# Rows of x and W1 ordered by head: y turned by matmuls of 96 and 32 columns, and sent SBUF to SBUF into x from the fourth group on

## The chip, the cores and the metric

The kernel runs on one core of one Trainium2 chip. The metric is the device time of one execution in microseconds; the time before is 962.65 us, the median of three runs (960.43 to 962.67).

## What is computed

A recurrence with complex decay, for 4 batches, 8 heads, 768 steps and a head width of 48, feeds a mixture of four dense experts whose outputs are all summed with normalised weights:

```python
S_re, S_im = (new_re + kv, new_im)                 # per step t: state times a[t], plus k[t] v[t]^T
y[:, :, t] = np.einsum('bhd,bhde->bhe', q[:, :, t], S_re)
...
x = np.ascontiguousarray(attn_out.transpose(0, 2, 1, 3)).reshape(B * S, H * D)      # 3072 x 384
...
for e in range(E):                                 # E = 4, w1[e] is 384 x 1024, w2[e] 1024 x 384
    h = np.maximum(x @ w1[e], 0.0)
    out += p[:, e:e + 1] * (h @ w2[e])
```

A feature of x is (head, place in the head): 8 x 48 = 384, which fill NJ = 3 blocks of 128 partitions on the chip. The order of the features within x is free as long as the rows of W1 follow it.

## The kernel before

Everything is split by time into NG = 12 groups of G = 256 steps, each of CG = 2 chunks of C = 128. The kernel has two stages.

**First stage.** For each group, `front` prepares queries and keys on the vector engine (DVE) and the scalar engine (ACT), and `send` moves them between partitions by DMA, the pieces of 16 partitions on POOL's queue and the others on SP's. The attention of a group (`near_attention` for groups 0 and 1, `attention` after that) is matmuls in chunked form; its result y has 112 partitions, in which a pair of heads lies at partitions 0 to 47 and 64 to 111, four pairs (HP) beside each other. While that goes on, `moe1` runs the first two experts for the group before, in eight steps of `w1_step` and `w2_step`. The pieces are woven together by hand in `between` and `advance`: a group's attention is taken up at steps `FIRST` to `end`, and `hold` keeps the sends of the next group's queries back until then. What is not pinned by `behind` and `keep_in_program_order` a planner orders, over the whole kernel, by simulated times.

y has to become x: 128 features on the partitions in three blocks, split into a high and a low part (`split_x`, L229: xh on ACT, xl on DVE), which `w1_step` (L246) multiplies with W1. There are two ways:

- For groups 0 to 2 (g < XSEL = 3), `turn_x` (L700 to L710) does it by matmul: for each chunk and each block j the two pairs of heads that lie in the block are multiplied with a slice of `band`, a shifted identity, 128 columns wide, and added up in PSUM. `split_x` reads PSUM. y is stored to DRAM as well, by `store_y` (L749 to L752), in two DMAs, one for each half of the pairs.
- For groups 3 to 11, `store_y` writes y to `y_d[g]` in DRAM, and `load_x` (L224 to L226) reads it back into the tile x with 128 features on the partitions, which waits on SP until both stores have landed.

`band` is made at the start on POOL (L343 to L347: a memset and two affine selects). The tile x and `band` share one buffer.

**Second stage.** The other two experts read `y_d` (`load_x2`, L1126) in blocks of 768 steps and work on sums of blocks of x and W1 (a scheme with fewer products). Weights that it needs are partly prepared in the first stage and written to `late_d` (L824, L825). A slow general path for unusual inputs stands behind a flag and does not run here.

SP's queue and POOL's queue are worked off in order: a DMA whose input is not ready holds up those behind it. PE, ACT and DVE are each in order as well.

Of the kernel before, what the change touches and what calls it, by code (L numbers as in the profile page):

```python
# [8 lines left out]
F32 = mybir.dt.float32  # L9
F32R = mybir.dt.float32r  # L10
AF = mybir.ActivationFunctionType
ALU = mybir.AluOpType
# [3 lines left out]
B, H, S, D = 4, 8, 768, 48  # L16
HD = H * D
NT = B * S
E, F = 4, 1024
P = 128  # L20
NJ = HD // P
C = 128
G = 256
CG = G // C
NG = NT // G
GB = S // G
NF = E * F // P
FE = F // P
# [5 lines left out]
M = 112  # L34
IM = 64
# [14 lines left out]
HP = H // 2  # L50
# [8 lines left out]
XSEL = 3  # L59
# [2 lines left out]
STEP = {1: 4.2, 2: 4.2, 3: 4.2, 4: 4.2, 5: 4.2}  # L62
MORE = (1.5, 2.3, 0.5)
LATE = {NG - 1: (1, 2, 3, 4, 5, 6, 7), NG: (0,)}
HOFF = 96
ROWS = ((0, 48, (0, 1, 2), 0, 0), (48, 48, (0, 1, 2), 0, 3), (96, 32, (0, 1), 0, 6), (96, 16, (2,), 32, 6),
        (112, 16, (2,), 32, 7))
WIDE = 32 + P + 48
DMA_SCRATCH = 4096
XOF = (0, 1, 2, 3, 4, 5, 6, 7, 0, 8, 9, 6, 10, 11, 12, 13, 14, 15, 5, 9)  # L70
UNIT = (
# [54 lines left out]
def fast_path(ctx, tc, qkP, aP, vP, probsP, w, out, flag):  # L126
    nc = tc.nc
    const = ctx.enter_context(tc.tile_pool(name="const", bufs=1))
    wpool = ctx.enter_context(tc.tile_pool(name="wpool", bufs=NF1))
    moe = ctx.enter_context(tc.tile_pool(name="moe", bufs=2))  # L130
# [4 lines left out]
    wide = const.tile([P, WIDE], F32, name="wide")  # L135
    nc.gpsimd.memset(wide, 0.0)
    nc.gpsimd.affine_select(out=wide, in_=wide, pattern=[[-1, WIDE]], compare_op=ALU.not_equal, fill=1.0,
                            base=32, channel_multiplier=1)
# [82 lines left out]
            behind(ins, prev)  # L221
            prev = ins

    def load_x(g):  # L224
        x = moe.tile([P, NJ, G], F32, tag="x", name=f"xa{g}", bufs=1)
        nc.sync.dma_start(x, y_d[g].rearrange("(j p) t -> p j t", p=P))  # L226
        return [(slice(0, G), x)]

    def split_x(g, parts):  # L229
# [68 lines left out]
    with ExitStack() as c1:  # L298
# [38 lines left out]
        for t in Gs:  # L337
            nc.gpsimd.memset(t, 0.0)
        nc.gpsimd.memset(TA, 0.0)
        band = moe.tile([P, HOFF + P + IM + C], F32, tag="x", name="band", bufs=1)  # L340
        near_mask = band[:, HOFF + P + IM:]
        band = band[:M, :HOFF + P + IM]
        nc.gpsimd.memset(band, 0.0)  # L343
        nc.scalar.activation(near_mask, m_ps[:, 2], AF.Copy)
        for r0, base in ((0, HOFF), (IM, HOFF + D)):
            nc.gpsimd.affine_select(out=band[r0:r0 + D], in_=band[r0:r0 + D], pattern=[[-1, HOFF + P + IM]],
                                    compare_op=ALU.not_equal, fill=1.0, base=base, channel_multiplier=1)  # L347

        def landed_first(ins, prev):
            if prev is not None:  # L350
# [349 lines left out]
        def turn_x(g, c, y):  # L700
            xp = ps_a.tile([P, NJ, C], F32, tag="pa", name=f"xp{g}_{c}")
            for j in range(NJ):
                ps = [p for p in range(HP) if -HOFF < 2 * D * p - P * j < P]
                for p in ps:
                    o = HOFF - (2 * D * p - P * j)
                    ins = nc.tensor.matmul(xp[:, j, :], band[:, o:o + P], y[:, p, c * C:(c + 1) * C],  # L706
                                           start=(p == ps[0]), stop=(p == ps[-1]))
                    if g == 0 and c == 0 and p == ps[0]:
                        behind(ins, state["yl", g, 1])
            return slice(c * C, (c + 1) * C), xp  # L710

# [35 lines left out]
            rotate(g)  # L747

        def store_y(g, y):  # L749
            yv = y_d[g].rearrange("(p u d) t -> u d p t", u=2, d=D)  # L750
            for u in range(2):
                nc.sync.dma_start(yv[u], y[u * IM:u * IM + D])  # L752

        def attention(g, QK):
            y = small.tile([M, HP, G], F32, tag="y", name=f"y{g}", bufs=1)
            (turn0, _, inc0, sc0, val0), (turn1, _, inc1, sc1, val1) = (chunk(g, c, QK[1], y) for c in range(CG))
            turn0()
            sc1()
            sc0(joined=True)
            inc0(True)  # L760
            yield turn1()
            val0(True, begin=True)
            inc1(True)
            val1(True)
            t_factors(g)
            store_y(g, y)
            x = [turn_x(g, c, y) for c in range(CG)] if g < XSEL else load_x(g)
            rotate(g)
            yield x

# [113 lines left out]
        x = {}  # L884
# [456 lines left out]
def general_path(ctx, tc, qkT, aT, vt, probs, w, out):  # L1341
# [97 lines left out]
    with ExitStack() as c2:  # L1439
        sb = c2.enter_context(tc.tile_pool(name="g_sb2", bufs=1))  # L1440
        ps = c2.enter_context(tc.tile_pool(name="g_ps2", bufs=2, space=PSUM))
        wt = sb.tile([P, NF, 2 * HD], F32, name="g_w")
        for i in range(NF):
            nc.sync.dma_start(wt[:, i, :], w[i])
        NB = S // P
        for b in range(B):
            with tc.For_i(0, S, P) as t0:
                x = sb.tile([P, H, D], F32, name="g_x")
                nc.sync.dma_start(x, y_d[:, b, bass.ds(t0, P), :].rearrange("h t e -> t h e"))
                pr = sb.tile([P, E], F32, name="g_pr")  # L1450
                nc.sync.dma_start(pr, probs[b * S:(b + 1) * S, :][bass.ds(t0, P), :])
                prs = sb.tile([P, 1], F32, name="g_prs")
                nc.vector.reduce_sum(prs, pr, axis=mybir.AxisListType.X)
                nc.vector.tensor_scalar(prs, prs, 1e-9, None, op0=ALU.add)
                nc.vector.reciprocal(prs, prs)
                nc.vector.tensor_tensor(pr, pr, prs.broadcast_to([P, E]), op=ALU.mult)
                xf = x.rearrange("p h d -> p (h d)")
                xp = ps.tile([P, NJ, P], F32, name="g_xp")
                for j in range(NJ):
                    nc.tensor.transpose(xp[:, j, :], xf[:, j * P:(j + 1) * P], ident)  # L1460
                xs = sb.tile([P, NJ, P], F32, name="g_xs")
                nc.scalar.activation(xs, xp, AF.Copy)
                acc = sb.tile([P, HD], F32, name="g_acc")
                for e in range(E):
                    po = ps.tile([P, HD], F32, name="g_po")
                    for f in range(FE):
                        wi = wt[:, e * FE + f, :]
                        hp = ps.tile([P, P], F32, name="g_hp")
                        for j in range(NJ):
                            nc.tensor.matmul(hp, wi[:, j * P:(j + 1) * P], xs[:, j, :],  # L1470
                                             start=(j == 0), stop=(j == NJ - 1))
                        hs = sb.tile([P, P], F32, name="g_hs", bufs=2)
                        nc.scalar.activation(hs, hp, AF.Relu)
                        nc.tensor.matmul(po, hs, wi[:, HD:], start=(f == 0), stop=(f == FE - 1))
                    if e == 0:
                        nc.vector.tensor_scalar(acc, po, pr[:, e:e + 1], None, op0=ALU.mult)
                    else:
                        nc.vector.scalar_tensor_tensor(acc, po, pr[:, e:e + 1], acc, op0=ALU.mult, op1=ALU.add)
                ot = out[b * S:(b + 1) * S, :][bass.ds(t0, P), :].rearrange("(i s) d -> s i d", i=SEG)
                for s in range(CS):  # L1480
                    nc.sync.dma_start(ot[s], acc[s * SEG:(s + 1) * SEG, :])
# [62 lines left out]
```

## Time and profile before

| | before |
|---|---|
| median of three runs | 962.65 us (960.43 to 962.67) |
| profiled execution | 960.0 us, span 958.2 us |
| PE busy | 933.9 us, 97% of the span |
| PE weight loads busy (beside PE) | 908.3 us, 95% |
| DVE busy | 745.2 us, 78% |
| ACT busy | 483.0 us, 50% |
| POOL busy | 210.7 us, 22% |
| granted TensorE clock over the span | 0.999 of full speed |

Engine times overlap, so they do not add up to the span. PE's matmuls are pipelined: the time of one record includes its way through the engine, and records overlap, so the distance from start to start is the better measure of what one costs. Where rows are merged, the duration runs from the first start to the last end.

### The profile page before, as it was taken

The numbers are of one execution on the slowest core, as the hardware profiler recorded it, in microseconds if no ns is written. First come the engines' busy times: TensorE is split into PE (matmuls) and PEld (weight loads), VectorE is DVE, ScalarE is ACT, GpSimd is POOL, SyncE is SP. The second block draws the span as 40 slices with busy tenths as digits, with TensorE's granted clock in tenths as the row PEclk, the third lists the DMA queues.
The fourth block names the chain that finished last, engine by engine and source line by source line (L and its number), as shares of the span: only waits on it lengthen the run. The fifth ranks groups of instructions, "written<-read, shape, count | busy, mean of one in ns | idle before, by whom it ended". The sixth has DMA issues, their size and how long they took to land.

```text
span 958.2 us, 19409 instructions
## 1 busy us (share of the span) xinstructions
PE 933.9 (97%) x7388; PEld 908.3 (95%) x7388; DVE 745.2 (78%) x1630; ACT 483.0 (50%) x1030; POOL 210.7 (22%) x294
## 2 busy tenths in 40 slices
PE   5999999999999999999999999999999999999997
PEld 3899999999999999999999999999999999999997
DVE  7898989989989999888996577748485757666642
ACT  7766446363564736547343555635454554444430
POOL 6030111020211202111111036333424352322000
PEclk9999999999999999999999999999999999999999
DMA  9585264544535546353437799131514433131112
GB/s 314 171 172 139 60 159 89 150 99 142 149 96 129 129 138 156 117 135 109 117 109 226 269 316 275 50 121 38 148 57 144 162 85 102 50 99 51 50 50 78
DMA packets 75029, 125.73 MB, mean 131 GB/s; under 512 B 9600, under 2 KB 50224, under 8 KB 74928
## 3 DMA queue, kind: packets, MB, share of 16 engines
q1 hardware_dynamic: 60464, 94.69, 32.7%
q0 software_dynamic: 14464, 29.72, 13.3%
q8 instruction: 60, 0.98, 0.5%
q14 instruction: 41, 0.34, 0.1%
HBM read 75.94 MB, written 31.46 MB: 112 GB/s over the span
## 4 chain that ended last, share of the span: by engine, by line
PE 89%; DVE 6%; DMA 3%; ACT 2%; issue 1%; SPq 0%; ACTq 0%; DVEq 0%
PE ph L246 21%; PE pob L995 20%; PE po L267 19%; PE pb L995 17%; PE sc L635 3%; PE yp L667 2%; PE dp L611 2%; PE yp L677 2%; PE ktp L584 1%; DMA RX<-w 1%; PE sc L652 1%; DMA shi<-late_d 1%; DVE pf L446 1%; PE xp L706 1%; DVE xl L1001 0%
## 5 line engine op out<-in xcount | busy, mean ns | idle before, releaser
L995 PE MATMUL pob<-shi,hid 128*128 128x384 f32 x528 | 148.5, 335 | 0.5 <-DVE hid L1004 0.5
L267 PE MATMUL po<-whi,hh 128*128 128x384 f32 x384 | 129.7, 338 | 0.0
L267 PE MATMUL po<-wlo,hh 128*128 128x384 f32 x384 | 128.9, 336 | 0.0
L257 ACT ACTIVATE hh<-ph 128x512 fp32r<-128x512 f32 x96 | 57.2, 596 | 121.8 <-PE ph L246 117.5
L1007 POOL TENSOR_TENSOR Z<-Z 128x384 f32<-128x384 f32 x84 | 89.9, 1104 | 114.6 <-DMA Z<-y_d 57.0
L246 PE MATMUL ph<-xha,whi 128*128 128x256 f32 x576 | 103.8, 287 | 1.3 <-ACT xha L233 1.3
L246 PE MATMUL ph<-xla,whi 128*128 128x256 f32 x576 | 101.0, 283 | 2.0 <-DVE xla L235 2.0
L246 PE MATMUL ph<-xha,wlo 128*128 128x256 f32 x576 | 102.0, 284 | 0.0
L995 PE MATMUL pb<-xh,shi 128*128 128x384 f32 x291 | 97.1, 335 | 1.0 <-DVE pb L1001 1.0
L995 PEld LDWEIGHTS pob<-shi,hid 128*128 128x128 f32 x528 | 96.4, 188 | 1.2 <-DVE hid L1004 1.1
L995 PE MATMUL pb<-xl,shi 128*128 128x384 f32 x288 | 96.2, 334 | 0.0
L995 PE MATMUL pb<-xh,slo 128*128 128x384 f32 x288 | 96.2, 334 | 0.0
L246 PEld LDWEIGHTS ph<-xha,whi 128*128 128x128 f32 x576 | 85.9, 190 | 5.3 <-issue 2.4
L258 DVE SCALAR_TENSOR_TENSOR hl<-ph,hh 128x512 fp32r<-128x512 f32 x96 | 65.9, 687 | 31.0 <-ACT hh L257 30.3
L995 PE MATMUL pob<-slo,hid 128*128 128x384 f32 x264 | 88.2, 334 | 0.0
L267 PE MATMUL po<-whi,hl 128*128 128x384 f32 x384 | 85.2, 338 | 0.5 <-DVE hl L258 0.5
L246 PEld LDWEIGHTS ph<-xla,whi 128*128 128x128 f32 x576 | 82.8, 191 | 2.7 <-DVE xla L235 2.4
L246 PEld LDWEIGHTS ph<-xha,wlo 128*128 128x128 f32 x576 | 82.8, 190 | 0.4
L998 ACT ACTIVATE SN<-pb 128x384 f32<-128x384 f32 x96 | 47.4, 494 | 66.7 <-PE pb L995 59.4
L1001 DVE TENSOR_TENSOR xl<-Z,xh 128x384 fp32r<-128x384 f32 x104 | 59.2, 598 | 21.7 <-ACT xh L998 16.3
L998 ACT ACTIVATE hid<-pb 128x384 fp32r<-128x384 f32 x76 | 37.3, 491 | 71.9 <-PE pb L995 71.5
L267 PEld LDWEIGHTS po<-whi,hh 128*128 128x128 f32 x384 | 72.4, 189 | 0.3 <-ACT acc L775 0.2
(238 smaller groups left out, 2119.4 us busy)
## 6 DMA issues: line engine op xcount, KB each, us to landing
qk<-qkP SPq DMA_DIRECT2D x24, 384.0 KB, 4.0
acc_d<-acc POOLq DMA_DIRECT2D x24, 384.0 KB, 5.3
ACC<-acc_d SPq DMA_DIRECT2D x48, 192.0 KB, 3.2
A<-aP SPq DMA_DIRECT2D x22, 384.0 KB, 6.1
v<-vP SPq DMA_DIRECT2D x24, 288.0 KB, 3.0
Z<-y_d SPq DMA_DIRECT2D x16, 384.0 KB, 4.8
Qst<-Q SPq DMA_DIRECT2D x40, 145.1 KB, 3.9
Kst<-K SPq DMA_DIRECT2D x40, 144.0 KB, 3.8
```

What stands on the lines that cost most here:

```text
L246: ins = nc.tensor.matmul(ph[:, u, :], wt[:, j * P:(j + 1) * P], xt[:, j, :], start=(n == 0), stop=(n == 3 * NJ - 1))
L257: wts["hh"] = nc.scalar.activation(hh, ph, AF.Relu)
L258: nc.vector.scalar_tensor_tensor(hl, ph, 0.0, hh, op0=ALU.max, op1=ALU.subtract)
L267: nc.tensor.matmul(po[t], part[0][:, u, t * P:(t + 1) * P], wts[i][n][:, HD:], start=(i % FE == 0 and part[0] is hh and n == 0), stop=(i % ...
L611: ins = nc.tensor.matmul(d_ps[o:o + n, h, :], KT[:, c, h, o:o + n], vc[:, h * D:(h + 1) * D], start=True, stop=True)
L635: ins = nc.tensor.matmul(to, k, q, start=True, stop=True)
L667: ins = nc.tensor.matmul(yo, vc[:, vo:vo + n], scs[2 * c + h // 4][:, h % 4, :], start=True, stop=first)
L677: ins = nc.tensor.matmul(yo, st[:, o:o + n], Qc[:, o // D, :], start=False, stop=True)
L995: return tc.keep_in_program_order(nc.tensor.matmul(*args, **kw))
L998: return pin(nc.scalar.activation(dst, src, fn, scale=scale))
L1001: pin(nc.vector.tensor_tensor(dst, x, y, op=op))
L1007: nc.gpsimd.tensor_tensor(dst, x, y, op=op)
```

## The change

The features of x are put into a new order, and the rows of W1 into the same order on the host: block j begins with the 96 features of the j-th pair of heads, and its last 32 rows hold a part of the fourth pair. XROWS lists the pieces as (first row in y, rows, first and last pair, first row in x, block).

- `turn_x` now takes two matmuls for each block, one with 96 columns of `band` for the block's own pair, and one with 32 columns for the part of the fourth pair, each into its own partitions of PSUM and with nothing to add up. As before that is six for a chunk.
- For groups 3 to 11 y no longer goes through DRAM: `send_x` copies it by six DMAs from SBUF into the tile x, the two pieces of 16 rows on POOL's queue, the other four on SP's; x is then written to `y_d[g]` by one DMA from there, for the second stage. `load_x` is gone. `t_factors` stands behind the sends in the text.
- For groups 0 to 2 `store_y` needs six DMAs in place of two.
- `band` has another layout and is filled by six small copies on POOL out of an identity, in place of two affine selects; it is narrower.

```diff
+XROWS = ((0, 48, 0, 3, 0, 0), (64, 48, 0, 3, 48, 0), (0, 32, 3, 4, 96, 0), (64, 32, 3, 4, 96, 1), (32, 16, 3, 4, 96, 2),
+         (96, 16, 3, 4, 112, 2))
+XMAIN = 2 * D
...
-    def load_x(g):
+    def send_x(g, y):
         x = moe.tile([P, NJ, G], F32, tag="x", name=f"xa{g}", bufs=1)
-        nc.sync.dma_start(x, y_d[g].rearrange("(j p) t -> p j t", p=P))
+        for r, n, p0, p1, q, j in XROWS:
+            (nc.gpsimd if n == 16 else nc.sync).dma_start(x[q:q + n, j:j + p1 - p0, :], y[r:r + n, p0:p1, :])
+        nc.sync.dma_start(y_d[g].rearrange("(j p) t -> p j t", p=P), x)
         return [(slice(0, G), x)]
...
         nc.gpsimd.memset(band, 0.0)
         nc.scalar.activation(near_mask, m_ps[:, 2], AF.Copy)
-        for r0, base in ((0, HOFF), (IM, HOFF + D)):
-            nc.gpsimd.affine_select(out=band[r0:r0 + D], in_=band[r0:r0 + D], pattern=[[-1, HOFF + P + IM]],
-                                    compare_op=ALU.not_equal, fill=1.0, base=base, channel_multiplier=1)
+        for r, n, p0, p1, q, j in XROWS:
+            o = q if q < XMAIN else XMAIN + 32 * j + q - XMAIN
+            nc.gpsimd.tensor_copy(band[r:r + n, o:o + n], wide[r:r + n, 32 + r:32 + r + n])
...
             for j in range(NJ):
-                ps = [p for p in range(HP) if -HOFF < 2 * D * p - P * j < P]
-                for p in ps:
-                    o = HOFF - (2 * D * p - P * j)
-                    ins = nc.tensor.matmul(xp[:, j, :], band[:, o:o + P], y[:, p, c * C:(c + 1) * C],
-                                           start=(p == ps[0]), stop=(p == ps[-1]))
-                    if g == 0 and c == 0 and p == ps[0]:
+                for p, q, o, n in ((j, 0, 0, XMAIN), (HP - 1, XMAIN, XMAIN + 32 * j, 32)):
+                    ins = nc.tensor.matmul(xp[q:q + n, j, :], band[:, o:o + n], y[:, p, c * C:(c + 1) * C],
+                                           start=True, stop=True)
+                    if g == 0 and c == 0 and j == 0 and q == 0:
                         behind(ins, state["yl", g, 1])
...
         def store_y(g, y):
-            yv = y_d[g].rearrange("(p u d) t -> u d p t", u=2, d=D)
-            for u in range(2):
-                nc.sync.dma_start(yv[u], y[u * IM:u * IM + D])
+            yv = y_d[g].rearrange("(j q) t -> q j t", q=P)
+            for r, n, p0, p1, q, j in XROWS:
+                nc.sync.dma_start(yv[q:q + n, j:j + p1 - p0], y[r:r + n, p0:p1])
...
-            t_factors(g)
-            store_y(g, y)
-            x = [turn_x(g, c, y) for c in range(CG)] if g < XSEL else load_x(g)
+            if g < XSEL:
+                t_factors(g)
+                store_y(g, y)
+                x = [turn_x(g, c, y) for c in range(CG)]
+            else:
+                x = send_x(g, y)
+                t_factors(g)
             rotate(g)
```

The general path and the host code follow the new order; neither is part of the time.

## Rows read from the trace of the kernel before

**Rows 1.** The page's part 4: shares of the chain that ended last, by engine
```profile
PE 89%; DVE 6%; DMA 3%; ACT 2%; issue 1%; SPq 0%; ACTq 0%; DVEq 0%
```

**Rows 2.** Table by stretch: length, PE, PE loads, DVE, ACT, POOL busy, clock, DMA
```profile
195.00:240.00 45.00, 45.00 (x450) 43.88 (x450) 40.48 (x89) 23.68 (x51) 5.39 (x10) 1.00 0.45 120
...
500.00:545.00 45.00, 45.00 (x422) 43.77 (x422) 29.60 (x73) 20.42 (x46) 3.40 (x6) 1.00 0.71 231
```

**Rows 3.** Chain in order of time, then PE's timeline (start, length), 187 to 195 us
```profile
187.57 3.06 DMA y_d<-y
...
190.77 3.22 DMA xa<-y_d
...
193.38 0.86 PE L267 MATMUL po<-whi,hl 128*128 128x384 f32 x4
...
194.91 0.62 PE L246 MATMUL ph<-xha,whi 128*128 128x256 f32 x3 [0.68 <-ACT xha L233]
```

**Rows 4.** Line 706 (ns min/median/max), then PE's timeline of the first group's turn
```profile
L706 PE MATMUL xp<-y,band x72: 272/275/377, 47.0 to 148.4; 112*128 112x128 f32 x72
...
47.04 0.49 PE L706 MATMUL xp<-y,band 112*128 112x128 f32 x2
...
47.04 2.94 PE L706 MATMUL xp<-y,band 112*128 112x128 f32 x24
```

**Rows 5.** PE's timeline just before that turn: two of a run
```profile
46.28 0.39 PE L677 MATMUL yp<-Qst,Gs 112*48 112x128 f32 x4
46.50 0.39 PE L667 MATMUL yp<-scs,v 128*48 128x128 f32 x4
```

**Rows 6.** PE's timeline at the end of the second group's turn
```profile
101.54 0.61 PE L706 MATMUL xp<-y,band 112*128 112x128 f32 x4
102.08 0.26 PE L611 MATMUL dp<-v,KT 128*64 128x48 f32 x2
```

**Rows 7.** Weight loads (PEld), then PE's timeline, around 32-wide matmuls of the setup
```profile
29.38 0.37 PEld L478 LDWEIGHTS qp<-Q,wide 128*32 128x32 f32 x16 [0.18 <-issue]
...
29.52 0.50 PE L478 MATMUL qp<-Q,wide 128*32 128x128 f32 x12
29.95 0.61 PE L220 MATMUL to<-whi 128*128 128x384 f32 x2
```

**Rows 8.** Weight loads by line and shape: count, busy us, mean ns
```profile
L706 PEld LDWEIGHTS xp<-y,band 112*128 112x128 f32 x72 | 8.5, 192 | 0.3 <-issue 0.3
...
L478 PEld LDWEIGHTS qp<-Q,wide 128*32 128x32 f32 x12 | 0.4, 109 | 0.2 <-issue 0.2
```

**Rows 9.** PE's timeline behind the turns of the first and second group
```profile
50.56 0.62 PE L246 MATMUL ph<-xha,whi 128*128 128x256 f32 x3 [0.58 <-ACT xha L233]
...
103.14 0.62 PE L246 MATMUL ph<-xha,whi 128*128 128x256 f32 x3
```

**Rows 10.** Timelines of DVE, ACT and PE in the third group
```profile
135.22 1.08 DVE L646 TENSOR_TENSOR scs<-sc,maskp 128x256 f32<-128x256 f32 x3 [0.68 <-PE sc L635]
...
152.33 0.55 DVE L235 TENSOR_TENSOR xla<-xp,xha 128x384 fp32r<-128x384 f32 x1
...
148.70 0.49 ACT L233 ACTIVATE xha<-xp 128x384 fp32r<-128x384 f32 x1 [2.44 <-PE xp L706]
...
152.93 0.39 PE L246 MATMUL ph<-xla,whi 128*128 128x256 f32 x1 [1.99 <-DVE xla L235]
```

**Rows 11.** Line 553 (issue ns min/median/max) and SP's sends of K, us to landing
```profile
L553 SPq DMA_DIRECT2D Kst<-K x60: 503/590/1893, 124.9 to 505.6; - x60
...
DMA to landing us min/median/max: 1.7/3.5/6.3
...
Kst<-K SPq DMA_DIRECT2D x20, 64.0 KB, 3.6
```

**Rows 12.** POOL's timeline from 172 to 200 us
```profile
199.42 1.00 POOL L553 DMA_DIRECT2D Qst<-Q  x2 [25.96 <-PE po L267]
```

**Rows 13.** POOL's timeline of the setup
```profile
10.94 1.26 POOL L346 TENSOR_SCALAR_AFFINE_SELECT band<-band 48x288 f32<-48x288 f32 x2
```

More of the change, by code (lines that the diff above doesn't have):

```diff
@@ L339, in fast_path @@
         nc.gpsimd.memset(TA, 0.0)
-        band = moe.tile([P, HOFF + P + IM + C], F32, tag="x", name="band", bufs=1)
-        near_mask = band[:, HOFF + P + IM:]
-        band = band[:M, :HOFF + P + IM]
+        band = moe.tile([P, XMAIN + NJ * 32 + C], F32, tag="x", name="band", bufs=1)
+        near_mask = band[:, XMAIN + NJ * 32:]
+        band = band[:M, :XMAIN + NJ * 32]
         nc.gpsimd.memset(band, 0.0)
         nc.scalar.activation(near_mask, m_ps[:, 2], AF.Copy)
-        for r0, base in ((0, HOFF), (IM, HOFF + D)):
-            nc.gpsimd.affine_select(out=band[r0:r0 + D], in_=band[r0:r0 + D], pattern=[[-1, HOFF + P + IM]],
-                                    compare_op=ALU.not_equal, fill=1.0, base=base, channel_multiplier=1)
+        for r, n, p0, p1, q, j in XROWS:
+            o = q if q < XMAIN else XMAIN + 32 * j + q - XMAIN
+            nc.gpsimd.tensor_copy(band[r:r + n, o:o + n], wide[r:r + n, 32 + r:32 + r + n])
         def landed_first(ins, prev):
@@ L1447, in general_path @@
             with tc.For_i(0, S, P) as t0:
-                x = sb.tile([P, H, D], F32, name="g_x")
-                nc.sync.dma_start(x, y_d[:, b, bass.ds(t0, P), :].rearrange("h t e -> t h e"))
+                x = sb.tile([P, HD], F32, name="g_x")
+                for r, n, p0, p1, q, j in XROWS:
+                    for p in range(p0, p1):
+                        o = (j + p - p0) * P + q
+                        nc.sync.dma_start(x[:, o:o + n],
+                                          y_d[2 * p + r // IM, b, bass.ds(t0, P), :][:, r % IM:r % IM + n])
                 pr = sb.tile([P, E], F32, name="g_pr")
@@ L1456, in general_path @@
                 nc.vector.tensor_tensor(pr, pr, prs.broadcast_to([P, E]), op=ALU.mult)
-                xf = x.rearrange("p h d -> p (h d)")
                 xp = ps.tile([P, NJ, P], F32, name="g_xp")
                 for j in range(NJ):
-                    nc.tensor.transpose(xp[:, j, :], xf[:, j * P:(j + 1) * P], ident)
+                    nc.tensor.transpose(xp[:, j, :], x[:, j * P:(j + 1) * P], ident)
                 xs = sb.tile([P, NJ, P], F32, name="g_xs")
@@ L1522, in chunked @@
         return np.ascontiguousarray(np.concatenate([x, y], axis=1))
-    w1 = moe_w1.reshape(E, NJ, P, FE, P).transpose(0, 3, 2, 1, 4).reshape(NF, P, HD)
+    order = np.zeros((NJ, P), dtype=np.int64)
+    for r, n, p0, p1, o, j in XROWS:
+        for p in range(p0, p1):
+            order[j + p - p0, o:o + n] = (2 * p + r // IM) * D + r % IM + np.arange(n)
+    w1 = moe_w1[:, order.reshape(-1)].reshape(E, NJ, P, FE, P).transpose(0, 3, 2, 1, 4).reshape(NF, P, HD)
     w2 = moe_w2.reshape(NF, P, HD)
```

1 line of the change is left out of this document (removed).

## Prediction

> **What bounds the kernel now.** I read the chain of work that ended last first: it is the tensor engine (PE) for 89% of the span [rows 1]. So a change counts by what it adds to PE's instruction stream or takes out of PE's idle time. The table by stage comes second: from 195 us to 545 us PE has next to no idle time (two of its eight stretches are shown) [rows 2], so there a result that arrives earlier is worth nothing. What could be won lies before, and the timeline of PE names three pieces of it: 0.58 us behind the turn of the first group's y [rows 9], 1.99 us in front of the third group's xla [rows 10], and 0.68 us in front of the fourth group's x (g = 3), the first that goes through DRAM [rows 3]. The chain shows the way to that one: store of y to y_d 3.06 us, load of xa from y_d 3.22 us, split, matmul [rows 3]. The eight later groups go the same way, but no PE wait is left on it.
>
> The sum is made against the profiled execution, 960.0 us with a span of 958.2 us; the median of the timed runs is 962.65 us, to which I carry the difference.
>
> **1. The turn of y for the first three groups (turn_x).** Twelve matmuls a group before and after; the trace shows two records for each (72 for 36) [rows 4]. Each passes 128 columns of y, and that stays. What changes is the weight: 128 columns before, 96 and 32 in turn afterwards. The first group's 24 records take 2.94 us, 2.67 us from first start to last (2.94 less one record of 0.275): 0.21 for the first step (0.49 less 0.275) and 22 steps of 0.112 [rows 4].
>
> A narrower weight alone saves nothing: 48-wide records pass in twos, four every 0.22 us, which is 0.11 us for a pass of one column block, as for wide ones [rows 5]. But two things depend on width. Matmuls on disjoint column blocks run side by side [rows 5], and a change of block width costs time. The last 128-wide record of the second group's turn starts at 101.54 + 0.61 - 0.275 = 101.875 us and the first 64-wide one at 102.08: 0.205 us instead of 0.112 [rows 6]. From 32 back to 128 columns: the last narrow record starts at 29.52 + 0.50 - 0.273 = 29.75 us, the first wide one at 29.95, the second of those (0.337 us each) at 29.95 + 0.61 - 0.337 = 30.22, 0.27 us later where 0.17 is usual; the step in is 0.20, and the second some 0.10 too long [rows 7]. The turn's own first step, after 48-wide work, shows the same 0.21 instead of 0.112 [rows 4]. From 48 to 32 columns the weight loads pause for 0.18 us and wait for nothing [rows 7].
>
> The changed turn goes from 96 to 32 columns and back all the time. The trace has no 96-wide weight; I take it as a 128-wide one, since it covers more than one of the 64-wide halves. Then each pair costs 0.20 into the wide one, 0.18 to its second record (0.21 less what 32 columns fewer save in loading: 128 columns load in 192 ns and 32 in 109, so some 0.03) [rows 8], 0.205 into the narrow one and 0.11 to its second record: 0.695 us against 4 x 0.112 = 0.447, that is +0.25 a pair. From first start to last a group then takes 5 x 0.695 + 0.495 = 3.97 instead of 2.67 us: **+1.3 us**. Bounds: with the two of a pair side by side, twelve steps of 0.112 = 1.34, so -1.33 us; with the full 0.21 and the change to 32 as dear as the way back (0.10 more a pair), +2.1.
>
> The rows of these changes give the price without any page. The Trainium skill, "TensorEngine Tiling (Array Packing)", section "Tiling Modes", says that a change of the tiling mode, not just of the tile, drains TensorE, and it lists column modes of 128, 64 and 32 and none of 96; it gives no price. That rule speaks against this edit: by it every step between 96 and 32 is a drain. By the same section's other rule, that different tiles work in parallel, the group would come out at the lower bound. The trace agrees with the drain at the three places above.
>
> Where this lies. In the first group PE waits for xha right behind the turn [rows 9], so all of it is on the path (the change back to wide weights hides in that wait): +1.3. In the second, dp and then ph follow without a wait [rows 6, 9]: +1.3. PE then runs on to scores for which the vector engine waits 0.68 us [rows 10], so its later work moves along. In the third group PE idles 1.99 us for xla, and what sets that is the vector engine's own queue: xla comes at 152.33 us although xha began at 148.70 and took half a microsecond [rows 10]. A turn longer by 1.3 us in two halves, with 0.4 us to change back behind them, stays under 1.99, and xha would still be done by 151: 0, and +1.6 if that cover is gone. Sum of part 1: +2.6 us, bounds -2.7 and +5.8.
>
> **2. From the fourth group on (send_x).** Removed: two stores and a load one after the other. Added: four sends on SP's queue and two on POOL's, then a store out of x. The last half of y is there at 187.57 us, when the second store was issued; x landed at 190.77 + 3.22 = 193.99 [rows 3]. Afterwards three SP sends remain at 187.57. Sends of K, also SBUF to SBUF, take 0.59 us to issue on SP and land 3.6 us after issue [rows 11]. So the last goes out at 187.57 + 2 x 0.59 = 188.75 and lands at 192.35, 1.65 us earlier. xha and the way to PE took 0.9 us (193.99 to 194.91) and would be done at 193.3. PE's record before starts at 193.38 + 0.86 - 0.33 = 193.91 and has 0.17 us to run, so it wants x at 194.1: the wait goes, 1.0 - 0.17 = **-0.8 us**. Next late for PE is nothing near: the relu of that step stands behind xha on the scalar engine, and moves up with it. Bounds: -0.8, and +1.0 if the last send is as slow as the slowest of that line (6.3 us: 195.05, PE at 195.95) [rows 11]. For the eight later groups 0, covered by the time that their x lies ready; without that cover the same -0.8 to +1.0 each.
>
> The store out of x waits on SP for all six sends, to about 192.4, as the load waited for the stores to 190.77. Behind it is the next group's Q send, whose POOL part goes at 199.42 [rows 12]: 7 us of cover. In the last group the writes of late_d slip by the same 1.6 us, in a stage where PE waits for nothing [rows 2]. For the first three groups SP issues six stores instead of two, at most 4 x 0.59 = 2.4 us more; behind them is a load of v for a later chunk. t_factors only moves behind the sends in the text, on another engine: 0.
>
> POOL's queue is in order. Before the next group's Q send it idles 25.96 us, to 199.42 [rows 12]. The two sends of y should fall into that: they are written ahead of the Q send, which `hold` keeps back until the group is over. That is some 1 us on an idle engine.
>
> **3. Setup.** Two affine selects go (1.26 us on POOL from 10.94 us on) [rows 13], six small copies come: between 0 and 0.6 us each, so -1.3 to +2.3 us on POOL. The turn first reads band at 47.04 [rows 4], over 30 us later; 0. W1's rows are reordered on the host: 0.
>
> Sum: +2.6 - 0.8 = +1.8 us: 961.8 us for the profiled execution, and 962.65 + 1.8 = **964.5 us** against the median. That is +0.2%; about 0.3% (2.9 us) is what a measurement of this kernel can tell from no change.
>
> **The rivals.**
> *Side by side.* 96 and 32 columns are disjoint, like the pairs in [rows 5]. If a 96-wide weight leaves the last 32 columns free, the first two groups save 1.33 us each, the third nothing (its wait is the vector engine's), the fourth 0.8: -3.5, 959.2 us. Against it: no row here has a weight of over 64 columns run beside another.
> *Neither drain nor overlap.* PE's stream stays, only the fourth group's wait goes: -0.8, 961.9 us. Against it: the steps in [rows 6, 7].
> *The cover in the third group fails, and the fourth wins nothing.* +2.6 + 1.6 = +4.2, 966.9 us, slower. It decides when the second xha of that group ends after 152.33 us or the planner, which orders the whole kernel anew, puts xla elsewhere. Against it: 1 to 2 us of margin.
> *POOL's sends come late.* If they land behind the Q send in POOL's queue, x of the fourth group is complete no sooner than 199.42 + 2.0 + 3.5 = 204.9, and PE, which had it at 194.91, at 205.8: +10.9, with the turn +13.5, 976.2 us. It decides when their place is after 199.42. Against it: written first, and ready 11 us earlier.
>
> **How the numbers follow.** Forecast 0.62, side by side 0.09, neither 0.12, cover fails 0.12, POOL late 0.05. Around the forecast I leave 1.5 us for the planner's new order and the spread of the runs (960.43 to 962.67), so that a fifth of it ends over +2.9. Slower: 0.12 + 0.05 + 0.12 = 0.29. Faster: most of side by side and a little of neither: 0.12. Same: 0.59. The range takes in side by side below and the failed cover above, with some spread on each: 958.8 to 968.5 us.
>
> **What would show it.** The turn's 24 records in the first two groups: 4.0 us from first start to last speaks for the drain, 2.7 for neither, 1.4 for the overlap. In the third group PE's wait for xla should shrink to about 0.4 us and move nothing behind it. In the fourth, xha should start 1.6 us earlier against the matmuls around it, with no PE wait behind it. POOL should show two short issues within a microsecond or two of y. The forecast is wrong if the 96-wide records run beside the narrow ones, if a later group waits for its x, or if the new order opens a gap on PE elsewhere.

## The result and the profile after

The changed kernel takes **971.5 us**, the median of five runs (971.22 to 973.88), against 961.57 us for the kernel before in the same session: a ratio of 1.0108 with a 95% interval from 1.0092 to 1.0125. The forecast was +1.8 us, the result +10, far beyond the spread. Of all executions on record one, among the twelve of E12 below, took 1857.28 us; no trace shows why, and E12's range leaves it out. The profiled execution took 972.02 us with a span of 970.3 us, against 960.0 and 958.2.

The chain's shares in the changed kernel [rows 1]:

```profile
PE 84%; DVE 7%; ACT 3%; DMA 3%; issue 1%; SPq 1%; DVEq 0%; ACTq 0%
```

Its table by stretch, with the columns of [rows 2]:

```profile
195.00:240.00 45.00, 43.27 (x428) 40.33 (x424) 41.67 (x98) 23.71 (x52) 7.24 (x14) 1.00 0.50 126
500.00:545.00 45.00, 45.00 (x427) 43.78 (x426) 34.68 (x89) 20.29 (x47) 6.92 (x13) 1.00 0.61 179
```

PE's part of the chain fell from 89% to 84%: other engines and transfers now set the end for a longer time. The stretch from 195 us, which had no idle time on PE, has 1.73 us.

The turn as the group of its line [rows 4], ns min/median/max:

```profile
L708 PE MATMUL xp<-y,band x72: 272/284/351, 46.8 to 154.8; 112*96 112x128 f32 x36, 112*32 112x128 f32 x36
```

PE's timeline: the first group's turn [rows 4], its first two records and the two after those (from short windows of the same timeline), then the third group's turn with what follows it [rows 10]:

```profile
46.80 4.42 PE L708 MATMUL xp<-y,band 112*96 112x128 f32 x24
...
46.80 0.46 PE L708 MATMUL xp<-y,band 112*96 112x128 f32 x2
...
47.19 0.41 PE L708 MATMUL xp<-y,band 112*32 112x128 f32 x2
...
150.61 4.42 PE L708 MATMUL xp<-y,band 112*96 112x128 f32 x24
155.61 0.62 PE L250 MATMUL ph<-xha,whi 128*128 128x256 f32 x3 [0.58 <-ACT xha L237]
```

The 24 records take 4.42 us in place of 2.94 [rows 4], which is +1.48 us a group; 1.3 was forecast. In the third group they stand in one piece, and PE goes on behind it with xha as soon as that is there: the 1.99 us wait for xla that was to cover them [rows 10] is not there any more.

The fourth group [rows 3]: ACT's last piece of y.

```profile
195.63 1.21 ACT L685 ACTIVATE y<-yp 48x512 f32<-48x512 f32 x2 [3.82 <-PE yp L681]
```

SP's queue with the sends and the store out of x:

```profile
196.28 2.74 SPq L229 DMA_DIRECT2D xa<-y  x4
200.47 0.39 SPq L230 DMA_DIRECT2D y_d<-xa  x1
```

POOL's queue [rows 12]:

```profile
196.51 1.10 POOL L229 DMA_DIRECT2D xa<-y  x2 [19.38 <-ACT y L685]
```

The last send in the chain in order of time:

```profile
198.43 1.96 DMA xa<-y
```

And PE's timeline:

```profile
201.40 0.61 PE L250 MATMUL ph<-xha,whi 128*128 128x256 f32 x3 [1.25 <-ACT xha L237]
```

POOL's issues stand beside SP's, right behind y, and x has landed at 198.43 + 1.96 = 200.39: 3.55 us after the end of y (195.63 + 1.21), where it took 193.99 - 187.57 = 6.4 us before. The mechanism is there, and is better than forecast. Yet PE waits longer for it than before, 1.25 us against 0.68 [rows 3]: not because x is slower, but because PE comes to that place earlier in its other work. It is ready for x 3.3 us after the end of y (201.40 - 1.25 - 196.84), where it was 6.7 us before (194.91 - 0.68 - 187.57).

What has grown is the list of PE's waits (total, times, longest), here in the kernel before and then in the changed kernel, without the first wait of the span (9.8 and 9.6 us):

```profile
PE ph L246 <- DVE xla L235: 2.0, 1, 2.0
PE ph L246 <- ACT xha L233: 1.3, 2, 0.7
...
PE kp L601 <- ACT KT L588: 1.0, 2, 0.7
PE sc L652 <- ACT Kst L602: 0.8, 3, 0.3
...
PE qp L478 <- DVE Q L520: 0.2, 1, 0.2
```

```profile
PE ph L250 <- ACT xha L237: 2.4, 3, 1.3
PE sc L656 <- ACT Kst L606: 1.7, 4, 0.9
PE po L271 <- ACT acc L781: 1.5, 1, 1.5
PE kp L605 <- ACT KT L592: 1.5, 2, 1.2
PE sc L639 <- DMA Kst<-K: 1.3, 2, 1.1
...
PE qp L482 <- DVE Q L524: 0.9, 1, 0.9
```

The waits behind acc and for Kst<-K are new, the one for xla is down to 0.4 us, the others are longer. Only the first line of the second list waits for something that the edit computes. And work that nobody edited takes longer. The scores of one group, between two matmuls of the second expert layer and dp, in the kernel before and then in the changed kernel (PE's timeline):

```profile
216.96 2.91 PE L635 MATMUL sc<-Qst,Kst 112*64 112x128 f32 x64
219.80 0.62 PE L246 MATMUL ph<-xha,whi 128*128 128x256 f32 x3
...
222.15 1.13 PE L611 MATMUL dp<-v,KT 128*64 128x48 f32 x32
```

```profile
222.61 0.60 PE L250 MATMUL ph<-xha,whi 128*128 128x256 f32 x3
223.14 0.43 PE L639 MATMUL sc<-Qst,Kst 112*64 112x128 f32 x2
223.51 0.50 PE L250 MATMUL ph<-xha,wlo 128*128 128x256 f32 x2
223.94 1.57 PE L639 MATMUL sc<-Qst,Kst 112*64 112x128 f32 x30
225.44 0.39 PE L250 MATMUL ph<-xha,wlo 128*128 128x256 f32 x1
225.66 0.28 PE L250 MATMUL ph<-xla,whi 128*128 128x256 f32 x1
225.87 0.43 PE L639 MATMUL sc<-Qst,Kst 112*64 112x128 f32 x2
226.23 0.51 PE L250 MATMUL ph<-xla,whi 128*128 128x256 f32 x2
...
229.41 1.13 PE L615 MATMUL dp<-v,KT 128*64 128x48 f32 x32
```

The same 64 score and 18 ph records take 222.15 - 216.96 = 5.19 us in one order and 229.41 - 222.61 = 6.80 us in the other, where the scores are cut into pieces of 2 and 30, and each cut goes from 128 columns to 64 and back.

Summed over the span, with the distance of each PE record to the next put down to its tile and all above 0.33 us to idle time, the +12.1 us of the profiled execution are: xp (the turn) +4.9, idle +3.9, sc +2.0, ph +0.85, the second stage +0.5. Up to the first group's turn the instructions of PE stand as before; of the 6255 PE matmuls outside the turn 240 have another successor than in the kernel before. ACT and DVE are reordered more: 197 of 1018 and 408 of 1594 instructions have another successor.

### The profile page after: what moved, and what is told of

Same layout as the page of the kernel before. It is cut to its first block, busy times and chain, and to the rows that moved or that the text cites. A ratio compares the mean times of both kernels' runs of the same rounds, so it can differ in the third digit from the quotient of the medians.

```text
span 970.3 us, 19531 instructions
## 1 busy us (share of the span) xinstructions
PE 941.1 (97%) x7388; PEld 907.7 (94%) x7388; DVE 746.3 (77%) x1630; ACT 482.6 (50%) x1030; POOL 219.9 (23%) x316
## 4 chain that ended last, share of the span: by engine, by line
PE 84%; DVE 7%; ACT 3%; DMA 3%; issue 1%; SPq 1%; DVEq 0%; ACTq 0%
PE pob L1001 20%; PE ph L250 19%; PE po L271 17%; PE pb L1001 16%; PE sc L639 3%; PE yp L671 2%; PE dp L615 2%; PE yp L681 2%; PE xp L708 1%; PE ktp L588 1%; DMA Z<-y_d 1%; DVE xl L1007 1%; DMA Kst<-K 1%; DVE Z L1007 1%; PE sc L656 1%
```

## The experiments

**Theories.** *Order*: the turn costs what its records show and the sends save a little, as forecast; the rest is the new order that the planner gave the kernel. *Turn*: the width changes carry the loss in any order. *Sends*: the six transfers disturb others, and x is late.

The ratio behind each time goes by executions of the kernel before in the same session, whose medians lie between 961.24 and 961.70 us.

To tell the theories apart an order is held: each instruction of an engine gets an edge to the one before it in a list of the other kernel's order (no wait, only the place in the queue).

```diff
+def pin(tc):
+    for name, runs in ORDER.items():
+        traced = [i for i in tc.nc.cur_bb.bb.instructions if i.engine == getattr(mybir.EngineType, name)]
...
+        for a, b in zip(order, order[1:]):
+            tc.add_manual_dep(traced[b], traced[a].name, ...
```

**E1: all edits, old order on PE, ACT and DVE.** The code of the change with the list above taken from the kernel before.

> All of the change's edits, with the instructions of PE, ACT and DVE held in the order that they had in the kernel before (POOL and SP are planned freely). Theory 'order' (the turn costs what its records show, the rest of the loss is the planner's new order): 961.6 before, +1.48 us for each of the first two groups' turns, 0 to +1.6 for the third, whose cover of 1.99 us is there again, -0.7 for the wait in front of the fourth group's x: 963.9 to 965.5 us. Theory 'turn' (the width changes themselves carry most of the +10 us, in whatever order): 968 to 971. Theory 'sends' (the six sends disturb other transfers and x comes late): 968 to 971, with PE waits for x or Kst in the same places as in the changed kernel.

967.22 us (967.13 to 968.85), ratio 1.0069 [1.0056, 1.0082]: the time fits none of the three. The trace says why. Up to 545 us the kernel is 1.8 us behind the kernel before; then one place takes the rest, here on PE's timeline

```profile
570.62 0.44 PE L271 MATMUL po<-whi,hh 128*128 128x384 f32 x1 [4.13 <-ACT hh L261]
```

and on ACT's:

```profile
568.32 1.76 ACT L1004 ACTIVATE xh<-Z 128x384 fp32r<-128x384 f32 x4 [5.55 <-DMA Z<-y_d]
```

The held order has conversions of the second stage ahead of hh on ACT, and their load comes later than in the kernel before. Read so, this is what holding the order costs when SP's order is not held with it; E5 tests that.

**E2: no edit, the changed kernel's order.** The kernel before, with the same few lines and the list taken from the changed kernel.

> The kernel before, none of the change's edits, with the instructions of PE, ACT and DVE held in the order that the planner gave them in the changed kernel. Theory 'order': most of the loss comes without any edit: 971.5 less 2.96 to 4.5 us for the turns, plus 0.7 to 2.5 for x through DRAM: 967.5 to 970 us, with the new waits (Q at 27 us, po behind acc at 580 us) in the trace. Theories 'turn' and 'sends': 961 to 963, since neither the narrow weights nor the sends are there.

969.99 us (969.07 to 974.48), 1.0111 [1.0090, 1.0131]. **Without one line of the change the kernel loses 8.6 us**, from the order of three engines and what SP and POOL make of it. Of the two waits that were named, the one for Q is there (1.4 us), the one behind acc is not: it comes with the sends (E4). The largest piece is PE in front of the fourth group's x, which still goes through DRAM here; PE's timeline:

```profile
200.26 0.62 PE L246 MATMUL ph<-xha,whi 128*128 128x256 f32 x3 [4.30 <-ACT xha L233]
```

Behind that wait the granted clock is down for some time (table by stretch, the clock is the third number from the right):

```profile
195.00:200.00 5.00, 0.96 (x6) 0.63 (x4) 3.94 (x6) 0.63 (x1) 0.00 (x0) 1.00 0.31 99
200.00:204.00 4.00, 3.74 (x17) 3.74 (x18) 1.99 (x3) 2.51 (x5) 0.21 (x1) 0.61 0.00 0
204.00:208.00 4.00, 4.00 (x31) 4.00 (x31) 3.39 (x7) 2.52 (x6) 1.46 (x3) 0.97 0.64 97
```

The second of these stretches has 17 matmuls in place of 30 or so: part of the price is paid behind the wait.

**E3: 128-column turn with the sends, old order.**

```diff
...
-                for p, q, o, n in ((j, 0, 0, XMAIN), (HP - 1, XMAIN, XMAIN + 32 * j, 32)):
-                    ins = nc.tensor.matmul(xp[q:q + n, j, :], band[:, o:o + n], y[:, p, c * C:(c + 1) * C],
-                                           start=True, stop=True)
+                for p, o in ((j, 0), (HP - 1, P + P * j)):
+                    ins = nc.tensor.matmul(xp[:, j, :], band[:, o:o + P], y[:, p, c * C:(c + 1) * C],
+                                           start=(p == j), stop=(p != j))
...
```

> The change's order of features and its sends, but the turn with 128-column weights: two matmuls a block that add up, as before, in the order of before on PE, ACT and DVE. No width change is left in the turn. All theories but 'sends' give 961.6 less the 0.7 us of the fourth group's wait: 960.9 us, and the difference to the run with narrow weights in the same order is the price of the narrow turn, 3.0 to 4.5 us by the records, 7 or more by theory 'turn'. Theory 'sends': 967 or more, with waits behind x and Kst.

965.93 us (964.05 to 967.21), 1.0049 [1.0036, 1.0062]. The place at 564 us is there too (3.54 us for hh and 1.46 for hl), so the time as a whole says nothing of the sends. Behind these waits the granted clock falls as in E2 (table by stretch), and it is 0.55 in the next 4 us:

```profile
568.00:572.00 4.00, 2.54 (x11) 2.19 (x10) 4.00 (x9) 1.72 (x4) 0.32 (x1) 0.59 0.55 163
```

Up to 545 us the kernel is 1.1 us ahead of the kernel before.

**E4: 128-column turn with the sends, planned freely.** E3's diff, without the list.

> The same wide turn and sends, planned freely. Theory 'order': the planner makes a third order, so the time may lie anywhere from 960 to 970 us, and what it differs from the run with the order of before (960.9 expected) is the order's alone. Theory 'turn': as with the old order, 961 to 962. Theory 'sends': 967 or more.

961.09 us (960.31 to 963.19), 1.0002 [0.9993, 1.0011], and now the planner stays near the old order by itself: 42 matmuls of PE have another successor, not 240. So neither the sends nor the new order of features upsets the plan; the narrow turn does. E4, planned freely, is 0.95 us ahead of the kernel before at 545 us, and E3, with the list, 1.1: up to there the holding costs nothing by itself.

**E5: all edits, old order up to 540 us.** E1 with lists cut off ahead of the last group (3888 instructions of PE, 593 of ACT and 1080 of DVE are held).

> All of the change's edits, PE, ACT and DVE held in the order of the kernel before only up to about 540 us of it, so that the last group and the second stage are planned freely. In the two runs that held the whole order PE lost 6.6 us in one place (at 564 us, hh behind ACT, where ACT's held order had conversions of the second stage ahead that waited for a load). Theory 'order': this is the held order's fault and goes: the offset of +1.78 us against before that the first of those runs showed at 545 us stays, with 0 to 1.3 us in the last group: 963.1 to 964.5 us. Rival 'sends': the loss belongs to the sends and stays: 967 us or more.

964.25 us (963.49 to 965.85), 1.0029 [1.0019, 1.0040]. E1's loss at 564 us was the held order's. **With the old order the change costs about what its parts were forecast to cost**, 1.8 us up to 545 us and 2.6 by the medians (961.70 before); against the changed kernel as planned, 971.5 us, 7.2 us are the order's. In the third group the turn stands in two parts again, and PE's wait for xla is down from 1.99 us to

```profile
155.50 0.62 PE L250 MATMUL ph<-xla,whi 128*128 128x256 f32 x3 [0.45 <-DVE xla L239]
```

**E6: the three 96-column matmuls of a chunk first, then the three of 32.** Planned freely; PE's order outside the turn is that of the changed kernel but for 6 places.

```diff
-            for j in range(NJ):
-                for p, q, o, n in ((j, 0, 0, XMAIN), (HP - 1, XMAIN, XMAIN + 32 * j, 32)):
+            for q, n in ((0, XMAIN), (XMAIN, 32)):
+                for j in range(NJ):
+                    p, o = (j, 0) if q == 0 else (HP - 1, XMAIN + 32 * j)
```

> As the changed kernel, but each chunk's turn does its three matmuls of 96 columns first and its three of 32 after them: two changes of width a chunk, not six. Theory 'change of width costs' (each pair's 0.725 us is two changes): a chunk takes 0.20 + 0.19 + 4 x 0.112 into and in the wide ones and 0.20 + 0.13 + 4 x 0.112 in the narrow ones, 1.62 us in place of 2.17, 1.1 us a group and 3.3 us in all where the turns are on PE's path: 968.2 us, if the order elsewhere is that of the changed kernel. Rival 'narrow weights cost by themselves': no difference, 971.5 us.

969.62 us (968.01 to 970.65), 1.0077 [1.0063, 1.0091]. The turn's 24 records, on PE's timeline:

```profile
46.70 3.27 PE L709 MATMUL xp<-y,band 112*96 112x128 f32 x24
```

3.27 us in place of 4.42: four changes of width fewer in each chunk are worth 1.15 us a group, as the steps said (expected 1.1), and the narrow weights themselves cost nothing, since records of one width follow each other every 0.109 us. On the whole it is 1.9 us and not 3.3, since PE then waits 0.9 us longer in all for K's way into the scores (Kst<-K 2.2 us in place of 1.3).

**E7 and E8: the narrow turn in the second group alone, and in the first and third alone.** Both planned freely.

```diff
+                    narrow = g in (1,)
...
+                    narrow = g in (0, 2)
```

> Sends and feature order as in the change; the turn with 128-column weights in the first and third group and with 96 and 32 columns in the second group alone, all planned freely. Theory 'one turn tips the plan' (it is the second group's turn at which the planner leaves the old order for good): the changed kernel's order and its loss, less two turns of 1.48 us: 967.5 to 969 us. Rival 'each narrow turn brings its own share': 961.1 (the wide turn) plus a third of 10.4, 964.6 us. Rival 'only what the records show': 962.6 us.

> The counterpart: 96 and 32 columns in the first and third group, 128 in the second, planned freely. Theory 'one turn tips the plan': the order stays near that of before, so 961.1 + 1.48 for the first group and 0 to 1.5 for the third: 962.6 to 964.1 us. Rival 'each its own share': 961.1 + two thirds of 10.4 = 968 us.

966.83 us (966.40 to 968.48), 1.0056 [1.0043, 1.0070], and 966.61 us (966.16 to 968.06), 1.0052 [1.0038, 1.0065]. That one turn tips the plan has fallen: E8 has only 94 other successors on PE (E7 227) and loses as much, 5.5 us over E4 where its records account for 1.5 to 3. That each turn brings its own share has fallen too: it gave 964.6 and 968 us. How much the order differs is no measure of what it costs.

**E9: a longer turn without narrow weights.** Two of three blocks of each chunk are turned twice.

```diff
-            for j in range(NJ):
+            for j in (0, 1, *range(NJ)):
                 for p, o in ((j, 0), (HP - 1, P + P * j)):
```

> Sends and feature order as in the change, the turn with 128-column weights and no change of width in it, but longer: two of the three blocks of each chunk are done twice (20 matmuls a group in place of 12; the second time overwrites the first with the same values). By the step of 0.112 us, 16 records more are +1.8 us a group, a little more than the +1.48 of the narrow turn. All planned freely. Theory 'any longer turn moves the plan': 961.1 + 2 x 1.8 + 0.3 for the third group = 965.0 by the records, and 3 to 7 us more from a new order: 968 to 972. Rival 'it is something about the narrow weights': the order stays near that of the wide turn, 964.5 to 965.5.

968.68 us (967.92 to 972.33), 1.0085 [1.0068, 1.0102], in a third order (242 other successors). By its records 965.0 was due, so 3.7 us are the order's: a longer turn without narrow weights is enough for another plan, and for a loss. But the loss lies elsewhere. Up to 502 us E9 is 3.5 us behind E4 (+2.55 against -0.95, counted as in the table below), which is what its records cost. It loses another 0.9 us up to 580 us and 2.8 us more from there to 593 us, at the start of the second stage. The changed kernel has most of its loss before 502 us. So it is not shown that the length of the turn is what gives the changed kernel its costly order.

**E10: 128-column turn with the sends, in the changed kernel's order.** E3's diff with the list of E2.

> The wide turn with the sends, PE, ACT and DVE held in the order of the changed kernel. With the run of the kernel before in this order (969.99, y through DRAM) and the changed kernel (971.5, narrow turn) it splits the new order's cost. Theory: in the new order PE takes up the fourth group earlier against its other work, so the sends are worth 2.5 to 3.5 us there (before in this order waits 4.3 us for xha, the changed kernel 1.3) and all three narrow turns are on PE's path, 4.4 us: 967.0 us from either side. Rival 'the sends cost what they save': 970.

966.66 us (966.36 to 968.10), 1.0059 [1.0045, 1.0072]: as expected, and the step between E2 and the changed kernel.

**E11: E6's turn in the old order up to 540 us.** E6's diff with the lists of E5.

> The changed kernel with the three 96-column matmuls of each chunk first and the three 32-column ones after them, PE, ACT and DVE held to about 540 us in the order of before. With the widths changing in pairs, in the same order, the time is 964.25 us. The grouped turn's records take 2.99 us in place of 4.15 from first to last, so in the first two groups 2 x 1.15 us go, the third is covered: 962.0 us. Rival, the records tell nothing of the path: 964.2.

961.17 us (960.82 to 963.25), 1.0005 [0.9996, 1.0013]: 3.1 us under E5 by the medians, which are of two sessions, and 2.3 by the traces, at 502 as at 932 us. That is two turns.

**E12: the third group sent too.** E4 with one number changed.

```diff
-XSEL = 3
+XSEL = 2
```

> Wide turn for the first two groups only; the third group's y is sent SBUF to SBUF as the later ones' (no turn for it), planned freely. The turn's 24 records, 2.7 us of PE, go. The sends take 3.6 us from the end of y to x, about what the turn and the split in halves took, and in that place PE waited 2.0 us for xla. Theory: y is sent as soon as it is there, PE has other work to go on with for some of the time: 959 to 961 us, up to 2 us faster than the turn for all three (961.1). Rival: the wait only changes its name and PE waits 3 to 5 us for x: 961.5 to 963.

962.39 us (960.54 to 963.17), 1.0007 [0.9997, 1.0017], in the rival's range: PE waits for x what it no longer computes, on its timeline

```profile
149.57 0.62 PE L250 MATMUL ph<-xha,whi 128*128 128x256 f32 x3 [3.00 <-ACT xha L237]
```

and goes on at a lower clock (table by stretch):

```profile
150.00:154.00 4.00, 2.83 (x18) 2.60 (x17) 3.89 (x6) 0.82 (x2) 0.00 (x0) 0.64 0.72 181
154.00:158.00 4.00, 4.00 (x20) 4.00 (x20) 2.93 (x7) 1.37 (x3) 0.00 (x0) 0.51 0.02 4
```

The two can be told apart. At the first matmul that reads xla E12 is 0.47 us ahead of the kernel before (152.46 against 152.93) and E4 0.60 (152.33): the wait has taken the turn's place and won nothing. At 158 us E12 is 1.9 us behind, and these 2.4 us are the clock's. Its two executions with a mean granted clock of 0.999 took 960.54 and 960.83 us, the other nine, at 0.994 to 0.996, 960.75 to 963.17.

**E13 to E15: the second stage's first loads in the old order.** In every kernel with sends PE loses another 1.6 us or so behind 545 us. ACT's wait for Z is the sign: the four loads of Z, which the kernel before issues in a row, have loads of weights between them in E4 (SP's queue, before and in E4):

```profile
551.28 2.61 SPq L1134 DMA_DIRECT2D Z<-y_d  x4
```

```profile
551.79 1.22 SPq L1140 DMA_DIRECT2D Z<-y_d  x2
553.05 0.49 SPq L1123 DMA_DIRECT2D slo<-late_d  x1
...
555.11 1.49 SPq L1140 DMA_DIRECT2D Z<-y_d  x2
```

ACT's timeline, then PE's, in E4:

```profile
565.52 1.77 ACT L1004 ACTIVATE xh<-Z 128x384 fp32r<-128x384 f32 x4 [4.29 <-DMA Z<-y_d]
```

```profile
569.52 0.44 PE L271 MATMUL po<-whi,hh 128*128 128x384 f32 x1 [1.41 <-ACT acc L781]
```

The three runs are E4, E5 and E11 with fifteen of SP's loads held in their old order.

```diff
+LOADS = (130, 126, 125, 124, 123, 122, 129, 133, 132, 128, 121, 120, 127, 119, 131)
...
+    for a, b in zip(LOADS, LOADS[1:]):
+        tc.add_manual_dep(traced[1 - b], traced[1 - a].name, ...
```

> Wide turn and sends, planned freely but for fifteen loads on SP at the start of the second stage, which are held in the order of the kernel before (the four loads of Z ahead of the weights). Theory 'order of the loads': the offset against before that this kernel has at 545 us, -0.95 us, stays to the end: 960.4 us in place of 961.1, and ACT's wait for Z before 565 us is under 2 us. Rival 'the later y itself': 961.1 as without.

> All of the change's edits, PE, ACT and DVE held to 540 us in the order of before, and the fifteen loads of SP too. The offset at 545 us is +1.80 us. Theory 'order of the loads': it stays, 963.2 us in place of 964.25. Rival 'the later y itself': 964.2 as without.

> The same with the three 96-column matmuls of a chunk ahead of the three 32-column ones. Offset at 545 us -0.54 us. Theory: 960.6 to 960.9 us, in place of 961.2; no version of the change is likely to be faster than before by more than a microsecond, since only the fourth group's wait is there to be won.

961.98 us (960.02 to 962.67), 1.0005 [0.9997, 1.0014]; 963.22 us (962.26 to 964.42), 1.0024 [1.0015, 1.0033]; 961.09 us (960.33 to 961.82), 1.0000 [0.9991, 1.0009]. By the medians E14 is 1.0 us under E5 as expected, but their sessions' medians of the kernel before lie 0.5 us apart and the traces show 0.4 (+3.03 against +3.46 at 932 us); the two others gained nothing. ACT's wait for Z in E13 is 2.36 us in place of 4.29, where under 2 was expected. PE's wait behind acc is gone in all three, and another stands in its place, in E14's timeline of PE:

```profile
576.33 0.44 PE L271 MATMUL po<-whi,hh 128*128 128x384 f32 x1 [0.87 <-ACT hh L261]
```

From 545 us to the end E14 loses 1.3 us against the kernel before where E5 lost 1.7. So the order of the loads was a small part of it; what else makes the last group dearer with the sends stays open. E13's twelve times lie in two clusters, 960.0 to 960.6 and 961.9 to 962.7. Its profiled execution (961.97) has the lower clock behind the third group's wait for xla, which is 2.01 us there and 2.02 in E4, whose clock stays at 1.00 (table by stretch, E13):

```profile
150.00:154.00 4.00, 1.99 (x12) 1.78 (x11) 3.97 (x6) 0.74 (x1) 0.91 (x1) 0.84 0.64 91
154.00:158.00 4.00, 4.00 (x25) 4.00 (x24) 2.98 (x7) 2.17 (x5) 0.00 (x0) 0.74 0.06 12
```

Its ph matmuls go from 0.4 us ahead of the kernel before to 1.1 behind over that place. That this makes the two clusters fits the mean granted clock of every execution: 0.998 to 1.000 in the four shorter ones of E13, 0.996 to 0.998 in the eight longer, and in E4 0.999 in eight (up to 961.18 us) and 0.997 in three (from 962.14 us on). Where in the span the clock fell is seen only in the one that was profiled. So E13's median hides what the loads are worth: its four shorter executions lie around the 960.4 us expected. No version was found that beats the kernel before.

**All of it in one table**: start of a ph matmul (of the second stage in the last two columns), minus that of the same matmul in the kernel before, in us. The head gives the time before.

```
                          50.56  103.14  149.25  194.91  239.26  502.38  580.51  931.85
E4  wide, sends, own      -0.58   -0.59   -0.62   -1.45   -0.54   -0.95   -0.01   +0.66
E5  edits, old order      +1.14   +2.55   +4.21   +1.73   +2.16   +1.80   +2.46   +3.46
E11 grouped, old order    -0.04   +0.22   +0.73   -0.60   -0.19   -0.54   +0.32   +1.15
E2  no edit, new order     0.00   +1.81   +2.17   +5.35   +6.92   +9.89   +9.31   +9.65
E10 wide, sends, new      -0.38   +1.43   +1.80   +1.89   +2.70   +5.32   +6.07   +7.17
changed kernel            +1.24   +4.52   +6.37   +6.48   +7.28   +9.49  +10.82  +11.94
```

## Why the prediction was wrong, point by point

**What bounds the kernel**: right. PE's stream and its few gaps are what every run above moves; the granted clock behind long waits (E2, E3, E12, E13) comes to it, which the prediction does not have. The base of 962.65 us was the middle one of three times; five in the result's session gave 961.57, which is a small part of the miss.

**The turn (part 1)**: right in mechanism and nearly in size. The four steps of a pair are 0.203, 0.187, 0.202 and 0.134 us in the changed kernel, 0.725 in all where 0.695 was taken; the term that was too small is the second record of the narrow one (0.11). E6 shows that the price is the change: 3.27 us with two changes of width a chunk against 4.42 with six. The Trainium skill, "TensorEngine Tiling (Array Packing)", section "Tiling Modes", says that a change of the tiling mode drains TensorE. The trace agrees that a change costs, 0.20 us from the last record of one width to the first of the next; it does not show by what. Side by side never happened. In the old order E5 less E4 gives +1.72, +3.14, +4.83 and then, behind the third group's cover, +3.18 us; +2.75 stay at 502 us. Forecast: +1.3, +2.6, covered, +2.6.

**The sends (part 2)**: right in the old order where they act. From 149 to 195 us E4 gains 0.83 us on the kernel before (-0.62 to -1.45); 0.8 was forecast. By 502 us 0.33 of it is left. That E5 is then 1.80 us behind, which is the forecast to its digits, is partly luck: turn +2.75 for 2.6, sends -0.33 for -0.8, and -0.6 from the setup, where executions differ by half as much (E11 and E15, the same up to there, stand 0.3 us apart at the first ph). What was wrong is "the writes of late_d slip by the same 1.6 us, in a stage where PE waits for nothing": from 502 us to the end the five kernels of the table with sends lose 1.6 to 2.5 us, and E2, which has none, gains 0.2. That it is these writes, and not something else that comes with the sends, is not shown.

**The step that failed** is in "How the numbers follow": "around the forecast I leave 1.5 us for the planner's new order and the spread of the runs". The order is the largest term of all. By medians the changed kernel is made up of +8.6 us for the order alone (E2), -3.3 for the sends in it (E10) and +4.8 for three narrow turns in it (971.5 less 966.66); in the old order, or near it, the same edits are -0.3 (E4) and +3.2 (E5). The records bear the last two terms out: three turns of 1.48 us are 4.4. The order also changes what each edit is worth: it puts PE in front of the fourth group's x too early, so that sends which save 0.8 us from 149 to 195 us in one order save 3.1 us there in the other (E2 loses 3.18, E10 0.09), and it removes the third group's cover. The last of the prediction's own signs, "if the new order opens a gap on PE elsewhere", is what came.

**The rivals**: that the cover in the third group fails came true, by its second condition ("the planner, which orders the whole kernel anew, puts xla elsewhere"), and the fourth group won nothing, as that rival has it. Its 966.9 us were passed all the same. The mechanism that mattered was named there and then tied to one wait of 1.6 us, though every matmul, conversion and load behind the first turn was open to it. POOL's sends were on time.

What stays open: why the planner's other orders are all worse (E7, E8, E9 and the changed kernel lose some 2.5 to 9 us to them). The runs show that they cost, and by which waits and cuts, not why a narrow or a longer turn brings them.

## What to carry to other kernels

Where a planner orders the whole program, an edit has two prices, its own and that of the order it brings; the second was 2.5 to 9 us here, from edits of 1 to 5 us on PE. Hold the old order and run the edit in it, and run the new order without the edit: the two runs split the result, and show whether to drop the edit or to pin the order. Hold it only as far as the queues left free allow: held to the end it cost E1 some 3 us more than E5. If weights of two widths must alternate on PE, do all of one width first.

## What the runs showed of the hardware

A 96-column weight goes at the pace of a wide one: records of 96 columns follow each other every 0.109 us (E6), those of 32 too and those of 128 every 0.112, with 0.20 us into another width and 0.13 to 0.19 us for the record behind it. After a wait of 2.0 us in one place the granted clock stayed at 1.00 in one execution (E4) and fell to means of 0.84 and 0.74 in another (E13); after waits of 4.30 us (E2), of 3.54 and 1.46 us (E3) and of 3.00 and 1.17 us (E12) stretches of 0.61, of 0.59 and 0.55, and of 0.64 and 0.51 followed, the last of which is about the lower of its two levels, 1.2 GHz.
